# Output projection of a decode step: result on 16 rows of 112 columns, pairs batch first, more heads in the 448-wide sum

## The chip, the cores and the metric

The kernel runs on one core of a Trainium2 chip. A core has a matrix engine (TensorE, here PE; its weight loads are listed apart as PEld), a vector engine (VectorE, DVE), a scalar engine (ScalarE, ACT), a general engine (GpSimd, POOL) and an engine that mainly issues transfers (SyncE, SP). They run their own programs and meet at semaphores. Sixteen DMA engines move data between the memory outside the core (HBM) and the on-chip memory SBUF; matmuls write into PSUM, which has eight banks of 128 partitions by 512 fp32 columns. The metric is the device time of one execution in microseconds (us).

## The reference

Four sequences, one new token each, with a cache of 8192 keys and values for 8 key/value heads of width 256; two query heads share a key/value head, so there are 16 query heads. The model width is D = 448.

```python
xn = layernorm(x)                                        # x: 4 x 1 x 448
q = (xn @ wq)                                            # 448 x 4096: 16 heads of 256
scores = einsum("bhqd,bhkd->bhqk", q, k) * 256**-0.5     # k, v: 4 x 8 x 8192 x 256
o = einsum("bhqk,bhkd->bhqd", softmax(scores), v)
s = o.reshape(4, 1, 4096) @ wo                           # 4096 x 448
h2 = gelu(layernorm(xn) @ w3) @ w4                       # 448 -> 1792 -> 448
g = silu(xn + h2)
return x + s * g
```

The reference has another branch in the MLP, over shifted groups of channels. With one token per sequence every shift leaves only zeros, so it adds nothing and the kernel leaves it out. K and V are 268 MB in bf16; all else is about 10 MB.

## The kernel before, in words

**Pairs.** The 32 (batch, key/value head) combinations are worked on in 16 pairs of neighbouring heads of one batch (`where`, line 141, says which). A pair's K is 8 MB and lies in SBUF with 64 partitions for each head, 128 positions in each partition. PE transposes K in groups of eight 128x128 blocks (`f_t`, line 650), DVE and ACT copy the groups to `kT` (`evac`, line 348), PE multiplies them by the query (`f_s`, line 663), ACT takes the exponential (`exps`, line 372), and PE multiplies by V (`f_pv`, line 700). DVE divides by the sum of the exponentials and writes the attention output, transposed, to `OT_all` (`f_ot`, line 545), eight columns for each pair: two heads by two halves of the head's width by two query heads. The loop over the pairs runs with a delay: V of one pair is used while K of the next is worked on.

**Queues.** SP issues every large load in order (`prog_sp`, line 236): wq, w3, the first K, w4, the part of wo for heads 9 to 15, then K and V of the pairs, and at the end V of the last pair in five pieces and the rest of wo in the order of `LATE` (line 126): heads 0 and 1, 2 and 3, 4 and 5, 6 and 7, then head 8 in two halves. Loads wait for buffers by semaphores that DVE raises (`v_k`, `v_v`). w4 lies where wo's heads 0 to 8 come later, so those heads can't be loaded before the MLP is done (`v_w4`).

**The MLP** runs between the eighth and the ninth pair (`mlp`, line 633, on PE; `f_mlp`, line 491, on DVE). Its second matmul is summed in four column groups of PE at once; DVE copies the four partial sums to `ou_f` and PE adds them by two fp32 matmuls with a selection matrix `selb`, one for each 224 columns of the result. That gives the result's form: the first 224 columns on partitions 0 to 3, the others on partitions 32 to 35. x and the normalized x are copied to the same form (`x4`, `xn4`, line 501).

**The output projection** (`finish`, line 765). Each of the 16 heads has two halves of 128 rows in `wo_sb`. Heads 9 to 11 are multiplied 448 columns wide in four column groups (`f_ou`, line 734), DVE copies the four partial sums to `ou_f` (line 581), and PE adds them by `selb` into the result in PSUM bank `o_ps` (line 779) after the first piece of the last V. The other heads go straight to `o_ps` (`f_o`, line 745): two matmuls of 224 columns for each half of a head, one for each group of partitions. Heads 12 to 15 (from `ALONE`, line 732) need the last pair's attention output; heads 0 to 8 need their late weights. DVE then multiplies by the gate `sg4` (line 593), adds x (line 595), and SP and ACT each store one half.

## Time and profile before

| | us |
|---|---|
| median of 4 runs (652.62 to 652.96) | 652.75 |
| the profiled execution | 652.69 |
| its span, first to last instruction | 651.1 |

| engine | busy us | share of the span |
|---|---|---|
| PE matmul | 503.3 | 77% |
| PEld (weight loads) | 412.1 | 63% |
| DVE | 257.5 | 40% |
| ACT | 269.0 | 41% |
| POOL | 3.7 | 1% |

The DMA engines moved 279.13 MB, 429 GB/s over the span. Busy shares are averages over the span; what a change at the end is worth is read in the chain of work that ended last and in the timeline there. In the timeline a row has its start and its length in us, then the engine, the line, the operation, what it writes and reads, the shapes, and in brackets how long the engine had been idle and what ended that. "PEq" and "DVEq" are those engines' sequencers, which take the waits at line 321. The windows give for a stretch of time its length, the busy time of PE, PEld, DVE, ACT and POOL (in brackets the number of instructions), PE's granted clock, the mean busy share of the DMA engines and the rate in GB/s. Matmuls of different column groups run side by side, so their lengths overlap.

### The profile page before, as it was taken

Reading aid. Unit: us, or ns where it says so; the run is one execution under the profiler, and the core shown is the slowest. Engines: PE = TensorE matmul, PEld = TensorE weight load, DVE = VectorE, ACT = ScalarE, POOL = GpSimd, SP = SyncE. Lnnn points to the kernel's source line nnn. Section 1 sums busy time; section 2 is a strip of 40 time slices with the busy share of each in tenths; the row PEclk is TensorE's granted clock in tenths of the full one; section 3 lists DMA queues with packets and bytes.
Section 4 is the critical chain, followed back from the end, with each engine's and each line's share of the span. In section 5 each row is a group of like instructions: output and inputs, shape, how many; then the busy total and the mean of one; then the engine's idle time right before and its main releaser. Section 6 shows DMA issues by size and latency. Waiting matters only on the chain. (4 is left out here: it accounts for less than half of the span.)

```text
span 651.1 us, 22042 instructions
## 1 busy us (share of the span) xinstructions
PE 503.3 (77%) x9699; PEld 412.1 (63%) x9699; DVE 257.5 (40%) x507; ACT 269.0 (41%) x361; POOL 3.7 (1%) x18
## 2 busy tenths in 40 slices
PE   2979979595877958588589868959597695959856
PEld 1876959294774928568277765919477392856824
DVE  7434535252442525335154343515244252433511
ACT  6634626062542605345144543606344260543510
POOL 2000000000000000000000000000000000000000
PEclk9778989697996969889689898969799796988968
DMA  9999999999999999999999999999999999999997
GB/s 387 443 421 424 439 431 451 419 440 429 437 447 407 463 407 459 409 453 431 423 448 413 457 413 439 441 427 443 423 443 443 411 455 415 443 427 433 453 405 302
DMA packets 10801, 279.13 MB, mean 429 GB/s; under 512 B 1060, under 2 KB 3240, under 8 KB 3752
## 3 DMA queue, kind: packets, MB, share of 16 engines
q1 hardware_dynamic: 10776, 278.99, 99.5%
q8 instruction: 7, 0.11, 0.1%
q14 instruction: 2, 0.02, 0.0%
q10 hardware_dynamic: 16, 0.01, 0.0%
HBM read 278.99 MB, written 0.00 MB: 428 GB/s over the span
## 5 line engine op out<-in xcount | busy, mean ns | idle before, releaser
L658 PE MATMUL pst<-ident_b,kn 128*128 128x128 bf16 x4096 | 304.6, 222 | 26.9 <-PEq L321 25.5
L355 ACT ACTIVATE kT<-pst 128x1024 bf16<-128x1024 bf16 x224 | 226.4, 1023 | 122.6 <-ACTq L321 122.5
L353 DVE COPY kT<-pst 128x1024 bf16<-128x1024 bf16 x288 | 197.8, 692 | 178.6 <-DVEq L321 178.6
L658 PEld LDWEIGHTS pst<-ident_b,kn 128*128 128x128 bf16 x4096 | 242.1, 99 | 28.9 <-issue 28.9
L671 PE MATMUL psc<-qc,kT 128*128 128x4 bf16 x4096 | 174.1, 165 | 6.3 <-PEq L321 5.8
L703 PE MATMUL psv<-vb,pT 128*8 128x512 bf16 x1024 | 103.6, 503 | 92.9 <-PEq L321 92.9
L671 PEld LDWEIGHTS psc<-qc,kT 128*128 128x128 bf16 x4096 | 153.4, 97 | 34.6 <-issue 34.2
L379 ACT ACTIVATE pT<-psc,negb 64x128 bf16<-64x128 f32 x64 | 28.4, 535 | 236.6 <-ACTq L321 236.3
L703 PEld LDWEIGHTS psv<-vb,pT 128*8 128x8 bf16 x1024 | 24.9, 94 | 125.9 <-issue 115.3
L514 DVE TENSOR_REDUCE rmax<-psc 64x2 f32<-64x256 f32 x32 | 13.5, 422 | 130.9 <-DVEq L321 130.7
L696 PE MATMUL psm<-sel,po 128*128 128x4 f32 x136 | 18.4, 258 | 1.4 <-PEq L321 1.4
L696 PEld LDWEIGHTS psm<-sel,po 128*128 128x128 f32 x136 | 17.3, 196 | 1.5 <-issue 1.5
L379 ACT ACTIVATION_READ_ACCUMULATOR pT<-psc,negb 64x1 f32 x64 | 16.4, 256 | 0.0
L543 DVE COPY po<-psv 128x512 f32<-128x512 f32 x17 | 11.8, 692 | 9.4 <-DVEq L321 9.4
L535 DVE COPY negb<-psm 128x4 f32<-128x4 f32 x16 | 2.6, 162 | 30.1 <-DVEq L321 30.1
L524 DVE TENSOR_REDUCE gmax<-psm 2x2 f32<-2x128 f32 x16 | 4.5, 278 | 20.5 <-DVEq L321 20.5
L367 ACT ACTIVATE vb<-pT 128x5000 bf16<-128x5000 bf16 (+2 forms) x3 | 10.6, 3568 | 0.1
L684 PEld LDWEIGHTS psm<-diag,ones_f 2*128 2x128 f32 x32 | 4.7, 182 | 7.0 <-issue 7.0
L680 PEld LDWEIGHTS psm<-ident_f,rmax 128*2 128x2 f32 x16 | 1.3, 81 | 12.3 <-issue 12.3
L603 PE MATMUL pst<-ident_b,xn_b 4*128 4x4 bf16 x14 | 0.6, 161 | 9.4 <-DVE xn_b L428 9.3
L603 PEld LDWEIGHTS pst<-ident_b,xn_b 4*128 4x128 bf16 x14 | 0.5, 95 | 10.3 <-issue 9.3
L703 PE MATMUL psv<-kn,pT 128*8 128x512 bf16 x58 | 5.6, 514 | 1.3 <-PEq L321 1.3
(93 smaller groups left out, 88.5 us busy)
## 6 DMA issues: line engine op xcount, KB each, us to landing
kn<-in_A_k_cache_dram SPq DMA_DIRECT2D x30, 4096.0 KB, 26.4
kn<-in_A_k_cache_dram SPq DMA_DIRECT2D x4, 2048.0 KB, 16.3
vb<-in_A_v_cache_dram SPq DMA_DIRECT2D x2, 4096.0 KB, 20.3
kn<-in_A_v_cache_dram SPq DMA_DIRECT2D x1, 4096.0 KB, 27.7
vb<-in_A_wq_dram SPq DMA_DIRECT2D x1, 3584.0 KB, 11.1
kn<-in_A_v_cache_dram SPq DMA_DIRECT2D x1, 2048.0 KB, 26.2
wo_sb<-in_A_wo_dram SPq DMA_DIRECT2D x4, 448.0 KB, 26.7
vb<-in_B_w_dram SPq DMA_DIRECT2D x1, 1568.0 KB, 13.7
```

Of the source, the lines that this page charges most:

```text
L353: engine.tensor_copy(dst, src).then_inc(S["v_ev"], 1)
L355: engine.activation(dst, src, ACT.Copy).then_inc(S["a_ev"], 1)
L367: f = act.activation(t, pT[:, 0:1].broadcast_to([P, t.shape[1]]), ACT.Copy)
L379: ins = act.activation(pT[own, 0:NC2 * NR].rearrange("p (c n) -> p n c", n=NR)[:, n], psc[own, 0:NC2 * NR].rearrange("p (c n) -> p n c", n ...
L514: ins = v.tensor_reduce(rmax[own, :], psc[own, 0:NC2 * NR].rearrange("p (c n) -> p n c", n=NR)[:, t * REP:(t + 1) * REP], AX.X, ALU.max)
L524: v.tensor_reduce(gmax[:, :], psm[0:REP, 0:P].rearrange("p (s k) -> p s k", s=NS), AX.X, ALU.max).then_inc(S["v_s"], 1)
L543: v.tensor_copy(po[:, :], psv[:, 0:CP * DH]).then_inc(S["v_po"], 1)
L658: ins = pe.transpose(dst[:, n * P:(n + 1) * P], kn[:, t, GC * j + kl, half * P:(half + 1) * P], ident_b[:, :])
L671: ins = pe.matmul(psc[:, kk * NR:(kk + 1) * NR], kT[:, j % RING, n * P:(n + 1) * P], qc[:, :, half, :], start=(half == 0), stop=(half == N ...
L684: pe.matmul(psm[:, P:P + NR], ones_f[0:REP, :], diag[:, :], start=True, stop=True).then_inc(S["p_m2"], 1)
L696: ins = pe.matmul(psm[:, o:o + NR], po[:, i * DH + dh:(i + 1) * DH:NHALF], sel[:, i, 0:NR], start=(i == 0), stop=(i == CP - 1))
L703: ins = pe.matmul(psv[o:o + CP * NR, 0:CP * DH], pT[:, kk * NR:(kk + CP) * NR], src[:, kk:kk + CP, :].rearrange("p c d -> p (c d)"), start ...
```

## The change

The result now has 16 rows of 112 columns: 8 rows (batch by the two halves of 224 columns) on partitions 0 to 7 with the first 112 columns of each half, and 8 on partitions 32 to 39 with the others. Rows of one batch are neighbours. To steer a product to the right one of the two rows, the weights' columns are taken from `OT_all` with a zero column between each two batches' columns: starting at a batch's column, or one step before it. For that, pairs go batch first (pair i is batch i % 4, heads 2 * (i // 4) and the next), and a pair's eight columns in `OT_all` are followed by eight zeros. `selb` likewise has zero columns, and is taken at two offsets. x is loaded to the new form by two transfers on ACT's queue; the normalized x is added before the MLP's partial sums are added. Heads 0 to 3 and 12 to 15 join the 448-wide sum of heads 9 to 11; its copy and the fp32 sum come after them. Heads 4 to 8 go straight to the result, with four matmuls of 112 columns for each half of a head. Heads 6 and 7 are two loads.

```diff
-    LATE = ((0, 1), (2, 3), (4, 5), (6, 7), (8,))
+    LATE = ((0, 1), (2, 3), (4, 5), (6,), (7,), (8,))
     def where(i):
-        return NS * i // HKV, NS * i % HKV
+        return i % Bn, i // Bn * NS
...
+        def ot(hq, dh, m, n=None):
+            k, t = divmod(hq // REP, NS)
+            at = first + k * Bn * NSL * PW + t * TW + dh * REP + hq % REP
+            step = PW
+            if n is None:
+                step = NSL * PW
+            else:
+                at -= n * PW
+            return OT_all[:, at:at + (m - 1) * step + 1:step]
+
+        def sel_sum(n):
+            return selb[:, NSL - 1 - n:NSL - 1 - n + PQ]
+
+        def split(dram, tile, i):
+            return (dram.rearrange("b (s n) -> (b s) n", s=NSL)[:, i * DS:(i + 1) * DS],
+                    tile[i * PQ:i * PQ + NSB, :])
...
         def store(eng, i):
-            eng.dma_start(out2d[:, i * DQ:(i + 1) * DQ], out_b[i * PQ:i * PQ + Bn, :]
-                          ).then_inc(S["dout"], 16)
+            eng.dma_start(*split(out2d, out_b, i)).then_inc(S["dout"], 16)
...
                 c(act.activation(st[:, col + 2:col + 3], st[:, col + 1:col + 2], ACT.Sqrt))
+                for i in range(NDG if k == 2 else 0):
+                    act.dma_start(*split(x2d, x4, i)[::-1]).then_inc(S["dx4"], 16)
...
-            c(v.tensor_reduce(selb[:, :], ident_f[:, :].rearrange("p (j r) -> p r j", j=NQD),
-                              AX.X, ALU.add))
+            c.sync()
+            c(v.tensor_reduce(selb[:, NSL - 1:NSL * Bn + NSL - 1:NSL], ident_f[:, :].rearrange(
+                "p (j r) -> p r j", j=NQD)[:, 0:Bn], AX.X, ALU.add))
...
-                c(v.tensor_copy(
-                    qT[:, :, :, dh, hh].rearrange("p b (a i) -> p i a b", a=NHF),
-                    qt_ps[:, m * P:(m + 1) * P].rearrange("p (i n) -> p i n", i=NQD)[
-                        :, :, 0:NHF * Bn].rearrange("p i (a b) -> p i a b", a=NHF)))
+                for t in range(NS):
+                    c(v.tensor_copy(
+                        qT[:, :, :, t, dh, hh].rearrange("p (a j) b -> p j a b", a=NHF),
+                        qt_ps[:, m * P:(m + 1) * P].rearrange("p (j s n) -> p s j n", s=NS, j=NQD // NS)[
+                            :, t, :, 0:NHF * Bn].rearrange("p j (a b) -> p j a b", a=NHF)))
...
-                v.tensor_copy(ou_f[:, :], h2_ps[:, 0:D]).then_inc(S["v_h2"], 1)
-                for src, dst in ((x_f, x4), (xn_f, xn4)):
-                    for i in range(NDG):
-                        ins = v.tensor_copy(dst[i * PQ:i * PQ + Bn, :],
-                                            src[:, i * DQ:(i + 1) * DQ])
-                ins.then_inc(S["v_s"], 1)
+                v.tensor_copy(ou_f[:, :], h2_ps[:, 0:D]).then_inc(S["v_s"], 1)
                 take(v, "v_s")
+                v.tensor_tensor(ou_f[0:Bn, :], ou_f[0:Bn, :], xn_f[:, :], ALU.add
+                                ).then_inc(S["v_h2"], 1)
+                v.wait_ge(S["dx4"], 16 * NDG)
                 take(v, "p_hs")
-                v.tensor_tensor(bout[:, :], hs_ps, xn4[:, :], ALU.add).then_inc(S["v_w"], 1)
+                v.tensor_copy(bout[:, :], hs_ps).then_inc(S["v_w"], 1)
...
-                    OT_all[:, bass.ds(at, PW)].rearrange("p (s a r) -> p a s r", s=NS, a=NHALF),
+                    OT_all[:, bass.ds(at * NSL, PW)].rearrange("p (s a r) -> p a s r", s=NS, a=NHALF),
...
             turned(NH * TW).then_inc(S["v_ot"], 1)
-            take(v, "p_ou")
-            v.tensor_copy(ou_f[:, :], ou_ps[:, 0:D]).then_inc(S["v_a"], 1)
             f_rz()
...
                 :, :, 0:NR]).then_inc(S["v_ot"], 1)
+            take(v, "p_ou")
+            v.tensor_copy(ou_f[:, :], ou_ps[:, 0:D]).then_inc(S["v_a"], 1)
             v.wait_ge(S["p_o"], 1)
-            c(v.tensor_tensor(res[:, :], o_ps[0:DP, 0:DQ], sg4[:, :], ALU.mult))
+            c(v.tensor_tensor(res[:, :], o_ps[0:DP, 0:DS], sg4[:, :], ALU.mult))
...
+            def f_sums(dst, start, stop):
+                for n in range(NSL):
+                    for i in range(NDG):
+                        at = n * DQ + i * DS
+                        ins = pe.matmul(dst[i * PQ:(i + 1) * PQ, 0:DS], sel_sum(n),
+                                        ou_f[:, at:at + DS], start=start and n == 0,
+                                        stop=stop and n == NSL - 1)
+                return ins
...
+            SUMMED = [hq for hs in LATE[:2] for hq in hs]
+            NOU = (HQ - NLATE + len(SUMMED)) * NHALF
+            nth = []
             def f_ou(hs):
                 for hq in hs:
                     for dh in range(NHALF):
-                        k = (hq - NLATE) * NHALF + dh
-                        o = k % NCG * CGW
-                        ins = pe.matmul(ou_ps[o:o + PQ, 0:D], OT[:, hq // REP, hq % REP, dh, :],
+                        k = len(nth)
+                        nth.append(hq)
+                        o, m = k % NCG * CGW, PQ if k < NCG else Bn
+                        ins = pe.matmul(ou_ps[o:o + m, 0:D], ot(hq, dh, m),
                                         wo_sb[:, hq, dh, :], start=(k < NCG),
...
-                        for i in range(NDG):
-                            ins = pe.matmul(o_ps[i * PQ:(i + 1) * PQ, 0:DQ],
-                                            OT[:, hq // REP, hq % REP, dh, :],
-                                            wo_sb[:, hq, dh, i * DQ:(i + 1) * DQ], start=False,
-                                            stop=stop and hq == hs[-1] and dh == NHALF - 1)
+                        for n in range(NSL):
+                            for i in range(NDG):
+                                at = n * DQ + i * DS
+                                ins = pe.matmul(o_ps[i * PQ:i * PQ + NSB, 0:DS],
+                                                ot(hq, dh, NSB, n),
+                                                wo_sb[:, hq, dh, at:at + DS], start=False,
+                                                stop=stop and dh == NHALF - 1 and n == NSL - 1)
...
-                f_ou(range(NLATE, ALONE)).then_inc(S["p_ou"], 1)
+                f_ou(range(NLATE, ALONE))
...
-                    if i == 0:
-                        take(pe, "v_a")
-                        for n in range(NDG):
-                            pe.matmul(o_ps[n * PQ:(n + 1) * PQ, 0:DQ], selb[:, :],
-                                      ou_f[:, n * DQ:(n + 1) * DQ], start=True, stop=False)
...
                 take(pe, "dwl0", 16)
-                f_o(LATE[0])
+                f_ou(LATE[0])
                 take(pe, "v_ot")
-                f_o(range(ALONE, HQ))
-                for i in range(1, len(LATE) - 1):
+                f_ou(range(ALONE, HQ))
+                take(pe, "dwl1", 16)
+                f_ou(LATE[1]).then_inc(S["p_ou"], 1)
+                take(pe, "v_a")
+                f_sums(o_ps, True, False)
+                for i in range(2, len(LATE) - 1):
                     take(pe, "dwl%d" % i, 16)
                     f_o(LATE[i])
```

`first` is 32, two pairs' room ahead of the first pair's columns; NSL = 2, DS = 112, NSB = 8. `x4` is now bf16, `xn4` is gone, and `x4`, `sg4`, `res`, `bout` and `out_b` are 112 columns wide.

## The prediction

> **What bounds the kernel now.** I read the share of the DMA engines first, then the chain that ended last, then the timeline of the last 17 us, then where the last weights land.
>
> ```profile
> DMA  9999999999999999999999999999999999999997
> q1 hardware_dynamic: 10776, 278.99, 99.5%
> 647.50:648.00 0.50, 0.11 (x2) 0.14 (x4) 0.00 (x0) 0.00 (x0) 0.00 (x0) 1.00 0.17 56
> 648.00:649.00 1.00, 0.81 (x12) 0.53 (x11) 0.15 (x1) 0.00 (x0) 0.00 (x0) 1.00 0.00 0
> ```
>
> SP's queue keeps the DMA engines busy for 99.5% of the span, in every slice but the last; 278.99 MB stand against 651.1 us. Two windows near the end show the data stopping at about 648.0 us. So only three things can move the time: the rate of the stream, a hole in it, and the 3.1 us between the end of the data and the end of the span. The chain shows those:
>
> ```profile
> 647.89 0.94 PE pst L749 x12
> 648.83 0.02 issue
> 648.85 0.39 DVE res L593
> 649.27 0.38 DVE out_b L595
> ```
>
> ```profile
> 634.55 0.60 PE L739 MATMUL pst<-wo_sb,OT_all 128*32 128x448 bf16 x6 [0.46 <-PEq L321]
> 635.30 0.63 DVE L581 COPY ou_f<-pst 128x448 f32<-128x448 f32 x1 [0.89 <-DVEq L321]
> 638.69 0.47 PE L779 MATMUL pst<-ou_f,selb 128*32 128x224 f32 x2
> 639.00 0.36 PE L779 MATMUL pst<-ou_f,selb 128*32 128x224 f32 x2
> 644.21 0.35 PE L759 MATMUL pst<-pT,kn 128*128 128x32 bf16 x8
> 644.49 1.90 PE L749 MATMUL pst<-wo_sb,OT_all 128*32 128x224 bf16 x32
> 646.76 0.60 PE L749 MATMUL pst<-wo_sb,OT_all 128*32 128x224 bf16 x8 [0.36 <-PEq L321]
> 647.89 0.93 PE L749 MATMUL pst<-wo_sb,OT_all 128*32 128x224 bf16 x12 [0.53 <-PEq L321]
> 649.68 0.35 SPq L233 DMA_DIRECT2D out_dram<-out_b  x1
> ```
>
> These timeline rows give the prices: six 448-wide matmuls 0.60 us, the copy of the sum 0.63, two fp32 matmuls of 224 columns 0.67 from first start to last end (each is two passes), a 224-wide matmul 49 ns after the one before ((0.60 - 0.26) / 7; one alone lasts 259 ns), a 32-wide one 25 ns ((0.35 - 0.176) / 7). PE sits idle before each group at L749: it waits for weights. L312's two loads are issued at 638.03 and 640.03 and land 10.0 and 8.3 us later (longest and shortest in that line's answer), at 648.0 and 648.3; L299's last, heads 6 and 7, lands 17.2 us after 630.53, at 647.7, the one before at about 646.6. The last two of the twelve load their weights at 648.47, 0.1 us after the ten before them: **the end hangs on the landing of head 8's second half**.
>
> **The change, part by part.**
>
> 1. *The last landing.* The bytes are the same; heads 6 and 7 become two loads of 224 KB. Between L299's landings a 448 KB load takes 1.13 us, and L312's 112 KB 0.3, so 224 KB cost between 0.56 and 0.6: two are 0 to 0.07 us more. I take +0.03. SP issues one load more (0.4 to 0.5 us where it isn't held up); its last issue today lies 8.3 us ahead of its landing, so that is covered. The residual x comes as two 1.8 KB loads (16 rows of 224 B) on ACT's queue at about 12 us: at the stream's 429 GB/s 0.01 us, at worst 0.1 if they delay the slowest engine.
>
> 2. *PE behind that landing.* Four matmuls of 112 columns in place of two of 224. Two column groups run side by side; 112 columns stream in half of 224's time, and a pair of 224 takes 2 x 49 = 98 ns, so 112 columns fewer are 47 to 49 ns fewer: one lasts 259 - 47 = 212 ns. The last starts 50 to 75 ns after the first and ends 0.02 us earlier than now: -0.02, ends -0.05 and +0.1.
>
> 3. *Is PE free by then?* This is the step on which the forecast turns. Now PE has only direct matmuls here. The wait for DVE's copy of the sum, today after the first piece of V and met before PE comes to it, moves behind heads 2 and 3: all direct matmuls are queued behind it on PE, and DVE's last multiply behind those. DVE's own wait for the sum moves behind its last OT, with only that multiply after it. Heads 0 to 3 and 12 to 15 join the 448-wide sum: heads 0, 1 (4 matmuls), then, after DVE's last OT at 644.88, heads 12 to 15 (8), then heads 2, 3 (4), landed at 645.5 (618.41 + 27.1). The 16 cost less than today's 32 (1.90 us): by L739, four are 0.41 us from first start to last end. So the sum ends at 645.62 + 0.41 = 646.03. DVE starts 0.15 us later (today 635.15 to 635.30), copies 0.63, to 646.81; PE starts 0.15 after that (as in the MLP: copy ends 327.48, first matmul 327.62), at 646.96. Four fp32 matmuls of 112 columns stream as many columns as L779's two, behind which others may already start: 0.4 to 0.5 us, to 647.4. Then heads 4 to 7 and half of head 8 are 36 matmuls of 112 columns. Nothing in the trace is 112 wide in column groups. The ends: 25 ns (L759's step) and 49 ns (L749's). At 25 PE is done at 648.3, before the wait that ends at 648.47; at 49 at 649.2, with the last four at 649.6. I take 25 to 28: two groups need 24 ns each for 112 columns, loads of 8 weight columns (82 to 88 ns in L703's rows) are shorter than L759's (96), and those already fit in 25. So 0 on the path; the other end is +0.8.
>
> Here a page speaks against the change. The Trainium skill, "TensorE: Matmul & The Clock Gate", section "Back-to-back issue gap", puts a sustained pair of weight load and matmul at about 81 ns for 128 columns. By it PE would end at about 650.8, 2.0 us later than now, and the sum below would be 654.5. L749's 49 ns for 224 columns already undercuts that figure, so I don't go by it.
>
> 4. *DVE at the end.* Two operations on 64x224 (383 and 382 ns) become 64x112. A tensor-tensor of 128x56 takes 216 ns, so a column costs (383 - 216) / 168 = 1.0 ns and 112 columns 272: -0.11 each, -0.22. The ends: 0 (no gain) and -0.33 (both as at 56 columns; x4 is bf16 now).
>
> 5. *The store.* 8 rows of 224 B on each of SP and ACT in place of 4 of 448. From issue at 649.68 to the end of the span are 1.42 us. Rows doubled, bytes equal: +0.05, ends -0.05 and +0.2 (half the 0.35 us of issue again).
>
> 6. *Start.* DVE makes 8 small copies of qT for 4 (four end 0.69 us after the first starts, 19.44 to 20.13): +0.4 us. It is then idle until 21.70, when the first transposes come, which wait for K. ACT issues two loads more (0.28 to 0.56 us each) and its fills slide to 18.9; its first evacuation is at 22.5. Cost 0; with that cover gone it would meet the next: SP issues the next K at 33.20, while what is queued lands until 43.3 (3.63 + 39.7), some 8 us of cover with 2 us for engines that end early. `selb`'s extra wait and memsets end before x lands at 4.5.
>
> 7. *MLP in the middle.* DVE adds the normalized x (4x448, by L445's 0.38 and L418's 0.50 about 0.5 us) between the copy at 326.85 and PE's sum; four copies of 4x224 beside it go. PE, and the transposes queued behind it, come 0.6 to 0.7 us later; who waits is SP's next K, issued at 341.17. The V load of 322.65 runs until about 353: 10 us of cover, cost 0. The multiply of `at` on DVE's registers, 16 times, meets the same cover.
>
> 8. *Pair order.* Each load is as large and as contiguous as before; only its first address changes. The stream already jumps between the K and the V array twice per pair, and no slice shows a hole. K loads are issued at 180.10, 219.07, 257.42 and 296.13, 38.7 apart on average. I take 0; the ends have no nearer row than the windows of 20 us, which run between 412 and 454 GB/s, so a change of either sign can't be excluded; 0.2% either way is 0.09 us per pair.
>
> Also, 16 KB instruction fetches (7 on their queue, about 0.9 us each on one engine) may be one more or fewer: the one at 332 us made the landings around it 0.3 late. I take 0, ends -0.3 and +0.3.
>
> **Sum.** +0.03 - 0.02 + 0 - 0.22 + 0.05 = -0.16 us. The profiled execution took 652.69 (span 651.1 and 1.6 around it), the median shown 652.75; the same few tenths come off either: 652.75 - 0.16 = **652.6 us**.
>
> **Rivals.**
>
> *PE is behind.* The narrow matmuls keep L749's step, or the fp32 sum starts late. For it: PE stands idle from 646.0 to 646.9 while heads 4 and 5 land at 646.6, and afterwards has 40 matmuls where 20 are left now. Against it: L759's 25 ns. Time at 49 ns: +0.8 - 0.16 = +0.6, 653.4. It decides from about 30 ns a matmul (36 x 30 = 1.08 us, to 648.5).
>
> *The stream is slower in the new order* (the other side). One mechanism: the jump of a batch at each load costs the queue time. 0.1 us at each of 15 jumps is +1.5 - 0.16: 654.1. It decides from 0.09 us a pair; for it stands only that 20 us windows differ by a tenth; against it that the K/V jumps show no hole.
>
> *The stream ends earlier.* The engines end unevenly: the DMA share is 0.86, 0.56, 0.47 and 0.17 in the last four half microseconds, 0.97 us of idle engines. If other fetches or small loads even that out, up to -1.0 - 0.16: 651.6; with a faster stream less. Nothing in the change aims its bytes at single engines.
>
> *The narrow operations save nothing.* DVE's fixed part rules, and the doubled rows cost what they may: 0 + 0.2, 652.9.
>
> **How the numbers follow.** What a measurement here can tell from no change is about 0.2%, 1.3 us: faster ends at 651.4, slower begins at 654.1. The forecast with the rival of no saving has 0.56, its own range 652.2 to 653.0. PE behind: 0.20, of it 0.03 beyond 654.1. The slower stream: 0.13, 0.10 beyond. The earlier end: 0.11, 0.07 beyond. So faster 0.07, same 0.80, slower 0.13. Leaving out 0.1 at either end gives 651.6 to 654.1.
>
> **What would show it.** In the changed profile: L593's and L595's successors at 0.27 us; the copy of the sum at about 646.2 and the fp32 sum at 647.0; the last four matmuls alone, after an idle gap of PE that the last landing ends; that landing at 648.3 to 648.4; K issues 38.7 apart. Wrong would be: no idle PE from 647 on (PE behind); a DMA share under 9 or K issues further apart (the stream); a last landing off by over 0.3 us.

## Result and profile after

Before: 652.71 us, median of 62 executions (652.58 to 653.14). The changed kernel: 653.43 us, median of 41 (652.15 to 654.92), ratio 1.0009 [1.0005, 1.0013]. So the median is 0.1% slower, with the whole interval above 1, where 652.6, a little faster, was forecast. One thing must be known to read these numbers: the executions of the changed kernel lie in three groups, those of the kernel before in one, so its median goes with the shares of the groups.

```
                 executions   around
before           62           652.71   (652.58 to 653.14)
changed, first   19           652.41   (652.15 to 652.60)
changed, second   7           653.54   (653.33 to 653.67)
changed, third   15           654.45   (654.15 to 654.92)
```

The profiled execution of the changed kernel took 652.50 us with a span of 651.0, and belongs to the first group. On its page the stream is as dense as before:

```profile
DMA  9999999999999999999999999999999999999997
...
q1 hardware_dynamic: 10800, 278.99, 99.5%
q8 instruction: 7, 0.11, 0.1%
```

The windows at its end (length; busy time of PE, PEld, DVE, ACT, POOL with counts; PE's clock; DMA share; GB/s):

```profile
647.50:648.00 0.50, 0.50 (x27) 0.50 (x22) 0.00 (x0) 0.00 (x0) 0.00 (x0) 1.00 0.26 86
648.00:649.00 1.00, 0.90 (x25) 0.54 (x19) 0.03 (x1) 0.00 (x0) 0.00 (x0) 1.00 0.01 4
```

PE is busy throughout the half microsecond from 647.5, where it had 0.11 us of work before. The chain that ended last (start, length, what):

```profile
647.06 0.58 PE pst L655 x8
647.64 0.99 PE pst L781 x36
648.63 0.03 issue
648.65 0.29 PE pst L781 x4
648.94 0.02 issue
648.97 0.28 DVE res L611
649.25 0.02 issue
649.27 0.27 DVE out_b L613
```

It begins at the fp32 sum (`f_sums`, L655) and has all 40 direct matmuls (L781) in it; before, it began 0.9 us from PE's end. The timeline shows the same end with what is not on the chain:

```profile
645.38 0.74 PE L769 MATMUL pst<-wo_sb,OT_all 128*4 128x448 bf16 x12 [0.17 <-PEq L337]
646.29 0.62 DVE L609 COPY ou_f<-pst 128x448 f32<-128x448 f32 x1 [1.05 <-DVEq L337]
647.06 0.58 PE L655 MATMUL pst<-ou_f,selb 128*32 128x112 f32 x8 [0.93 <-PEq L337]
647.44 1.49 PE L781 MATMUL pst<-wo_sb,OT_all 128*8 128x112 bf16 x40
648.62 0.14 PEld L781 LDWEIGHTS pst<-wo_sb,OT_all 128*8 128x8 bf16 x4 [0.16 <-issue]
648.97 0.27 DVE L611 TENSOR_TENSOR res<-pst,sg 64x112 f32<-64x112 f32 x1 [2.06 <-PE pst L781]
649.56 0.37 SPq L250 DMA_DIRECT2D out_dram<-out_b  x1
```

This is the end that was forecast: 36 narrow matmuls are done when the last weights land at 648.52, and four follow them alone. Against before: the last landing is 0.15 later (648.37), PE's end behind it 0.04 shorter, DVE's two operations 0.23 shorter, the store the same 1.42 us; 0.15 - 0.04 - 0.23 = -0.12, which is what the span lost (651.10 to 650.98). The first of the four starts 240 ns after the last of the 36, where a matmul otherwise follows after 24.5, so PE has waited some 0.2 us; in the profile of e1_again below it is 61 ns, and PE and the landing come almost together. If the first group is like these profiles, the forecast's mechanism held in 19 of 41 executions. What the other 22 do, this profile can't show. The experiments had to find it.

### The profile page after: what moved, and what is told of

Same layout as the page of the kernel before. It is cut to its first block, busy times and chain, and to the rows that moved or that the text cites. A ratio compares the mean times of both kernels' runs of the same rounds, so it can differ in the third digit from the quotient of the medians.

```text
span 651.0 us, 22071 instructions
## 1 busy us (share of the span) xinstructions
PE 498.5 (77%) x9711; PEld 408.7 (63%) x9711; DVE 256.4 (39%) x508; ACT 268.6 (41%) x361; POOL 3.4 (1%) x18
## 5 line engine op out<-in xcount | busy, mean ns | idle before, releaser
L683 PE MATMUL pst<-ident_b,kn 128*128 128x128 bf16 x4096 | 301.5, 221 | 25.1 <-PEq L337 23.6
L683 PEld LDWEIGHTS pst<-ident_b,kn 128*128 128x128 bf16 x4096 | 239.6, 99 | 26.6 <-issue 26.6
L713 PE MATMUL psw<-rowsum,ones_f 128*128 128x4 f32 x34 | 6.7, 269 | 0.0
```

The costliest lines, as they stand in the source:

```text
L683: ins = pe.transpose(dst[:, n * P:(n + 1) * P], kn[:, t, GC * j + kl, half * P:(half + 1) * P], ident_b[:, :])
L713: pe.matmul(psw[:, 0:NR], ones_f[:, :], rowsum[:, :], start=True, stop=True).then_inc(S["p_s"], 1)
```

## Experiments

### What makes the groups: order of the pairs, x loads, or stores?

The first theories took three parts of the change that touch the queues: the new order of the pairs (theory O), the two small loads of x on ACT's queue with DVE's wait for them (theory X), and the stores with 16 rows of 224 B in place of 8 of 448 (theory S). Each was undone alone beside the changed kernel itself. These four share a before of 652.76.

**e1_again** is the changed kernel without an edit.

> The changed kernel as it is, for its spread. Its 43 executions so far lie in three groups: about 652.4 (21), 653.5 (7) and 654.5 us (15), while the kernel before stays within 652.58 to 653.14. I expect the three groups again, in about these shares. If the profiled execution falls in a slow group, its tail tells where the time is: theory X (the small x loads on ACT's queue hold up one DMA engine) expects the last landing 1 to 2 us after 648.5 and the rest as before; theory C (PE's clock is granted at half in the tail of some executions) expects a granted clock near 0.5 after 643 us and the last landing at 648.5; theory S (the stores of 224 B rows, which share lines of the output between the two queues) expects all as before up to 649.6 and a longer end.

Measured: 652.45 (652.30 to 653.78); nine of 11 executions in the first group, 653.55 and 653.78 in the second. The groups come in changing shares, and the ratio to before with them: 0.9998 [0.9989, 1.0007] here. None of these 11 lies in the third group. (The 43 that the expectation counts are the 41 above and two more of the first group.)

**e1_no_x_load** leaves the two loads and the wait out, so x isn't added.

```diff
-                for i in range(NDG if k == 2 else 0):
-                    act.dma_start(*split(x2d, x4, i)[::-1]).then_inc(S["dx4"], 16)
...
-                v.wait_ge(S["dx4"], 16 * NDG)
```

> The two x loads and the wait for them are left out, so x isn't added to the result. Theory X: one group alone, near 652.4. Theories C, S and O (the batch-first order disturbs the stream): the same three groups, median 653 to 654.

Measured: 652.55 (652.21 to 655.0); eight of 11 in the first group, three at 654.3, 654.42 and 655.0. The third group is there without the loads: theory X falls.

**e1_old_order** takes the pairs in the old order.

```diff
     def where(i):
-        return i % Bn, i // Bn * NS
+        return NS * i // HKV, NS * i % HKV
```

> The pairs' order of before with everything else of the change; queries and outputs then belong to other pairs than the keys, the work is the same. Theory O: one group, near 652.4. Theories X, C and S: three groups as in the changed kernel.

Measured: 652.98 (652.13 to 654.49); six of 12 in the first group, one at 653.42, five from 654.09 on. Theory O falls.

**e1_half_store** stores only the first 112 columns of each half; the rest of the result stays unwritten.

```diff
         def store(eng, i):
-            eng.dma_start(*split(out2d, out_b, i)).then_inc(S["dout"], 16)
+            eng.dma_start(out2d[:, i * DQ:i * DQ + DS], out_b[i * PQ:i * PQ + Bn, :]).then_inc(S["dout"], 16)
```

> Each store writes 4 rows of 224 B, 448 or more apart from the other store's (the other half of the output is left unwritten). Theory S: one group, near 652.4. Theories X, C and O: three groups as in the changed kernel, each at most 0.1 us earlier.

Measured: 653.94 (652.24 to 654.95); four of 12 in the first group, two in the second, six in the third. Theory S falls.

None of the three parts makes the groups. But the profiled execution of e1_old_order was one of the third group (654.09), and its timeline shows where the time goes:

```profile
644.95 1.82 PE L769 MATMUL pst<-wo_sb,OT_all 128*4 128x448 bf16 x16
646.93 0.62 DVE L609 COPY ou_f<-pst 128x448 f32<-128x448 f32 x1 [1.60 <-DVEq L337]
647.70 0.96 PE L655 MATMUL pst<-ou_f,selb 128*32 128x112 f32 x8 [0.93 <-PEq L337]
648.42 2.10 PE L781 MATMUL pst<-wo_sb,OT_all 128*8 128x112 bf16 x40
650.56 0.27 DVE L611 TENSOR_TENSOR res<-pst,sg 64x112 f32<-64x112 f32 x1 [3.00 <-PE pst L781]
```

Its last weights land at 648.31, earlier than in the profile after. Yet DVE's last multiply starts 1.59 us later. The sum's copy is 0.64 later (646.93 against 646.29), the direct matmuls start 0.72 after the fp32 sum instead of 0.38 (+0.34), and they take 2.10 instead of 1.49 (+0.61). A direct matmul comes (2.10 - 0.29) / 39 = 46.4 ns after the one before, where the other profile has 24.5. PE works at about half its rate; the copy on DVE takes the same 0.62. The windows, cut where the clock changes, say why (the figure behind the engines is PE's granted clock):

```profile
636.73:640.14 3.41, 3.41 (x36) 1.02 (x28) 0.20 (x1) 0.00 (x0) 0.00 (x0) 0.50 0.96 408
640.14:643.55 3.41, 1.89 (x34) 1.09 (x30) 0.69 (x1) 0.00 (x0) 0.00 (x0) 1.00 1.02 401
643.55:646.97 3.42, 3.22 (x31) 1.73 (x30) 0.20 (x2) 0.00 (x0) 0.00 (x0) 0.50 0.98 372
646.97:650.38 3.41, 2.68 (x48) 2.58 (x48) 0.59 (x1) 0.00 (x0) 0.00 (x0) 0.50 0.11 38
```

In all traces of this case the clock is either 0.5 or 1.0, and changes only at steps 3.41 us apart, whose place against the program's start differs from execution to execution (643.55 here, 644.35 in the profile after). The Trainium skill, "TensorE: Matmul & The Clock Gate", section "Part 1: The HAM clock gate", describes just this: two levels, decided by the array's activity in free-running windows of 3413 ns. The traces agree.

### Is it the clock?

The new theory: in some places of the steps, PE streams too little in one step of the changed tail, the clock halves, and the end runs at half speed. Its rival: PE is late for another reason, and the clock only goes with it. Two kernels keep PE busy or idle with nothing else changed; a third undoes the later sum. Before here: 652.85.

**e2_keep_busy** adds matmuls whose result nobody reads, where PE waits.

```diff
+            def f_idle(n):
+                for _ in range(n):
+                    pe.matmul(pst[2][:, 0:512], ident_b[:, :], kT[:, 0, 0:512], start=True, stop=True)
...
+                    f_idle(2 if i == 2 else 0)
                     take(pe, "dvl%d" % i, 16)
...
+                f_idle(2)
                 f_direct(NPIECE - ND)
...
                 f_ou(LATE[1]).then_inc(S["p_ou"], 1)
+                f_idle(3)
                 take(pe, "v_a")
```

> The changed kernel with seven matmuls of 128x512 into an unused PSUM bank while PE waits: two before the third piece of V, two before the fourth, three while DVE copies the sum. Theory C: the groups at 653.5 and 654.5 get rarer or vanish, the fast group stays near 652.4 (at half clock seven of them are 3.0 us, so some executions may lose some tenths). Any theory in which the clock is a bystander: the three groups stay as they are.

Measured: 652.57 (652.32 to 653.31), ratio to before 0.9997 [0.9988, 1.0006]; seven of 11 up to 652.57, four from 653.0 to 653.31, none near 654.4. That alone proves little, as e1_again had none there either; taken with the two runs below that fill the same three waits with less (e4_fill_113, e5_fill_113), one of 33 executions lies in the third group, against 15 of 52 of the changed kernel (41 and e1_again). More work on PE makes the group rare, which a PE that is late by its work can't explain. The fill has a price: the profiled execution (653.31) is at full clock from 641.56 on, yet its copy of the sum starts 1.12 us after that of the profile after (646.29):

```profile
644.00:648.00 4.00, 3.77 (x53) 2.23 (x51) 1.36 (x3) 0.00 (x0) 0.00 (x0) 1.00 0.81 305
647.41 0.62 DVE L609 COPY ou_f<-pst 128x448 f32<-128x448 f32 x1 [1.05 <-DVEq L337]
```

**e2_idle_after** leaves out the multiplication of the first three pieces of the last V but for four matmuls, so that PE stands idle for 3.88 us ahead of the third piece, which it reaches at 641.46 as in e1_old_order (641.40).

```diff
                     take(pe, "dvl%d" % i, 16)
-                    ins = f_pv(kv, PIECES[i], PIECES[i + 1], pb)
+                    if i == NPIECE - ND - 1:
+                        ins = f_pv(kv, 0, NCG * CP, NCG * CP)
```

> The same left out in the changed kernel. Theory C: nearly all executions in the slow groups, 653.3 to 655, median about 654.4. If the clock is a bystander: three groups with the shares of the changed kernel, about half at 652.4.

Measured: 654.54 (654.33 to 654.73), ratio 1.0026 [1.0016, 1.0036]. With less work all eight executions lie in the third group, and its windows show half the clock from 634.66 to the end:

```profile
634.66:638.07 3.41, 2.45 (x14) 1.56 (x13) 0.36 (x3) 0.80 (x5) 0.00 (x0) 0.50 0.96 411
638.07:648.00 9.93, 4.95 (x54) 3.05 (x56) 1.95 (x5) 0.00 (x0) 0.00 (x0) 0.50 0.93 366
648.00:651.00 3.00, 2.77 (x48) 2.50 (x48) 0.19 (x1) 0.00 (x0) 0.00 (x0) 0.50 0.00 0
```

Its last weights land at 648.37, no later than in the profile after. So the third group is the tail at half clock.

**e2_idle_before** is the same edit in the kernel before (same diff).

> The kernel before with its multiplication by the first three pieces of the last V left out but for four matmuls, so PE idles from about 635 to 641 us and comes into the tail at half clock in most executions. Theory C: the 52 matmuls of 224 columns keep PE busy enough to get the clock back, and 8 of 12 lie behind the landing at 647.8; 652.8 to 653.6, less than 1 us over the kernel before. If the kernel before never loses by half clock, 652.7.

Measured: 653.53 (653.13 to 654.79), ratio 1.0012 [1.0003, 1.0021]. In its profile (653.50) the clock is half from 635.22 to 648.88; the median is 0.7 us above before's. The kernel before is not immune to a low clock; it has less behind it at the end. Of its 236 executions in all series, one lies above 653.36 (e3_before below).

**e2_early_sum** takes the sum back to its old place, with heads 9 to 11 alone in it, and keeps the 16 rows.

```diff
-            NOU = (HQ - NLATE + len(SUMMED)) * NHALF
+            NOU = (ALONE - NLATE) * NHALF
...
                     ins = f_pv(kv, PIECES[i], PIECES[i + 1], pb)
+                    if i == 0:
+                        take(pe, "v_a")
+                        f_sums(o_ps, True, False)
...
-                f_ou(LATE[0])
+                f_o(LATE[0])
                 take(pe, "v_ot")
-                f_ou(range(ALONE, HQ))
-                take(pe, "dwl1", 16)
-                f_ou(LATE[1]).then_inc(S["p_ou"], 1)
-                take(pe, "v_a")
-                f_sums(o_ps, True, False)
-                for i in range(2, len(LATE) - 1):
+                f_o(range(ALONE, HQ))
+                for i in range(1, len(LATE) - 1):
```

> The change without its later sum: only heads 9 to 11 are summed 448 wide, copied and added where the kernel before does it; heads 0 to 3 and 12 to 15 go straight to the result with matmuls of 112 columns. Theory C (the granted clock: a profile in the slow group showed 0.50 from 643.6 to 650.4 us, changes 3.41 us apart, and the last landing not later) in its form 'the later sum thins PE's work between 643 and 647 us, so the gate keeps half the clock, and leaves more work behind it': one group near 652.4 to 652.5 or a spread of some tenths as in the kernel before. If instead the 16-row form is at fault (twice as many matmuls in the end), the three groups stay, median 653 to 654.5.

Measured: 653.97, 654.24, 666.28, 667.08, 667.14 and 671.65. This doesn't answer the question, as it brought a cost of its own. Its 104 direct matmuls in place of 40 make PE's program longer, and the page of the shortest execution counts ten instruction fetches of 16 KB in place of seven:

```profile
q8 instruction: 10, 0.16, 0.1%
```

One of them, at 647.6, falls into the end. The last weights land at 649.43, 0.9 us later than in the profile after, and the clock is full from 642.57 on. In the chain PE then stands for 0.55 us in "issue", waiting for nothing that the profile shows:

```profile
646.61 2.69 PE pst L781 x95
649.30 0.55 issue
649.85 0.56 PE pst L781 x9
```

That the fetches make the gap and the late landing is argued from the place of the one; for the 666 to 672 us of four other executions even that is missing, as none of them was profiled. How the 16 rows alone would do stays open.

### Which part of the change lowers the clock?

Now the later sum was put alone into the kernel before, and the fill of e2_keep_busy was split. Before here: 652.71.

**e3_late_sum**: heads 0 to 3 and 12 to 15 in the 448-wide sum, copy and fp32 sum behind them; result on 8 rows, old order, old stores.

```diff
-            take(v, "p_ou")
-            v.tensor_copy(ou_f[:, :], ou_ps[:, 0:D]).then_inc(S["v_a"], 1)
             f_rz()
...
-                    if i == 0:
-                        take(pe, "v_a")
-                        for n in range(NDG):
-                            pe.matmul(o_ps[n * PQ:(n + 1) * PQ, 0:DQ], selb[:, :],
-                                      ou_f[:, n * DQ:(n + 1) * DQ], start=True, stop=False)
...
-                f_o(LATE[0])
+                f_ou(LATE[0])
                 take(pe, "v_ot")
-                f_o(range(ALONE, HQ))
-                for i in range(1, len(LATE) - 1):
+                f_ou(range(ALONE, HQ))
+                take(pe, "dwl1", 16)
+                f_ou(LATE[1]).then_inc(S["p_ou"], 1)
+                take(pe, "v_a")
+                for n in range(NDG):
+                    pe.matmul(o_ps[n * PQ:(n + 1) * PQ, 0:DQ], selb[:, :],
+                              ou_f[:, n * DQ:(n + 1) * DQ], start=True, stop=False)
+                for i in range(2, len(LATE) - 1):
```

> One part of the change alone, on the kernel before: heads 0 to 3 and 12 to 15 join the 448-wide sum, whose copy and fp32 sum come after heads 2 and 3. Result still on 4 rows of 224 in two groups, pairs in the old order, 224-wide matmuls. Theory C with the later sum as its cause: groups appear, the fast one at 652.6 to 652.8, slow ones 1 to 2 us above. If the 16-row form is the cause: one group at 652.7 as in the kernel before.

Measured: 654.59 (652.58 to 655.31), ratio 1.0019 [1.001, 1.0029]; three of 11 around 652.6, two around 653.8, six from 654.59 on. All three groups come with this part alone. The windows of its profile (654.82):

```profile
639.93:643.34 3.41, 1.75 (x35) 0.79 (x27) 0.69 (x1) 0.00 (x0) 0.00 (x0) 1.00 1.02 401
643.34:646.75 3.41, 3.41 (x32) 2.50 (x32) 0.17 (x1) 0.00 (x0) 0.00 (x0) 0.50 1.00 381
646.75:650.17 3.42, 2.48 (x27) 1.77 (x22) 0.62 (x1) 0.00 (x0) 0.00 (x0) 0.50 0.13 46
```

**e3_wait_fill**: of the fill only three matmuls, ahead of the third piece of V.

```diff
+                    f_idle(3 if i == 2 else 0)
                     take(pe, "dvl%d" % i, 16)
```

> The changed kernel with three matmuls of 128x512 into an unused PSUM bank before the wait for the third piece of V (0.64 us at full clock), none elsewhere. If the gate drops at 643 to 644 us because PE waited through most of the 3.41 us before: the slow groups vanish or get rare, fast group 652.4, some executions 0.1 to 0.6 later. If the thin work after 644 us is what matters alone: the groups stay.

Measured: 653.41 (652.56 to 654.34), ratio 1.0012 [1.0003, 1.0021]; one of 11 at 652.56, six around 653.4, four around 654.2. Its profile (654.21) shows the thin step moved to the copy of the sum, 644.24 to 647.65:

```profile
640.83:644.24 3.41, 2.90 (x48) 1.16 (x41) 0.69 (x1) 0.00 (x0) 0.00 (x0) 1.00 1.03 399
644.24:647.65 3.41, 2.33 (x32) 1.55 (x32) 0.78 (x2) 0.00 (x0) 0.00 (x0) 1.00 0.86 322
647.65:651.06 3.41, 2.83 (x48) 2.58 (x48) 0.36 (x3) 0.00 (x0) 0.00 (x0) 0.50 0.01 4
```

**e3_copy_fill**: only two matmuls, while DVE copies the sum.

```diff
                 f_ou(LATE[1]).then_inc(S["p_ou"], 1)
+                f_idle(2)
                 take(pe, "v_a")
```

> The changed kernel with two such matmuls while DVE copies the sum, none elsewhere. The gate has dropped before that, so the groups stay in number; where the two make the stretch to 647 us dense enough for the clock to come back, the group at 654.5 moves towards 653.5. If the waits before 643 us don't matter: the groups vanish.

Measured: 652.79 (652.35 to 654.16), ratio 1.0003 [0.9994, 1.0012], spread from one end to the other. In its profile (653.17) the clock halves at 645.61 and is full again at 649.03.

**e3_before** is the kernel before as it is, to find its steps.

> The kernel before, for its profile. In its profile so far the clock's changes lay at 638.9, 642.3, 645.7 us and it stayed full. If this execution has changes near 640.1 and 643.5 (as the slow one of the changed kernel had): theory C expects half the clock from 643.5, full again at about 647, and a time within 0.5 us of 652.7.

Measured: 652.88 (652.40 to 654.06). In its profile (652.85) the steps lie at 641.65, 645.06 and 648.48, and the clock is full from the first on. Of eight executions one took 654.06, which stays unexplained.

No profile of the changed kernel itself fell into the second group; that it comes from a drop at a later step or a shorter one, as in e3_copy_fill, is argued, not shown. e3_wait_fill dropped later too, at 647.65, and took 654.21; e2_keep_busy took 653.31 at full clock. What makes the second group stays open.

So neither fill does it alone: the change leaves two thin places, the wait for the third piece, which the fp32 sum has left, and the copy of the sum.

### Does the kernel before meet the same steps?

One sub-theory was that the kernel before drops too and recovers in time. The second question was how little fill suffices. Before here: 652.82.

**e4_before_a** and **e4_before_b** are the kernel before as it is.

> The kernel before once more, for the clock of its tail. If the gate's steps fall near 640.1 and 643.5 us: either it drops there too and is full again at about 647 (then the dense matmuls of 224 columns give it back, and the time stays within 0.5 us of 652.7), or it doesn't drop (then the work to 643.5 differs).

> The same kernel, for another position of the steps: with steps near 644.3 and 647.7 us I expect full clock throughout, as in the changed kernel's fast profile.

Measured: 652.80 (652.65 to 653.07) and 652.75 (652.58 to 653.01). By luck e4_before_a has its steps where the third-group e1_old_order has them:

```profile
636.73:640.14 3.41, 3.41 (x38) 1.58 (x32) 0.57 (x2) 0.00 (x0) 0.00 (x0) 0.50 0.97 409
640.14:643.55 3.41, 2.24 (x37) 1.11 (x31) 0.69 (x1) 0.00 (x0) 0.00 (x0) 1.00 1.03 403
643.55:646.97 3.42, 3.04 (x52) 2.70 (x53) 0.17 (x1) 0.00 (x0) 0.00 (x0) 1.00 0.98 372
646.97:650.38 3.41, 1.29 (x20) 0.82 (x16) 0.77 (x2) 0.00 (x0) 0.00 (x0) 1.00 0.10 36
```

Same places, same clock until 643.55, and then 1.00 where e1_old_order has 0.50: here the kernel before doesn't drop, nor in its three other profiles (steps at 642.33, 641.65 and 639.79). So the sub-theory falls for these places of the steps; for others no profile shows it. Its timeline shows why the step from 640.14 has more in it:

```profile
638.47 0.59 PE L779 MATMUL pst<-ou_f,selb 128*32 128x224 f32 x2
...
638.84 0.59 PE L779 MATMUL pst<-ou_f,selb 128*32 128x224 f32 x2
638.91 1.80 PE L703 MATMUL psv<-kn,pT 128*8 128x512 bf16 x14
641.44 0.81 PE L703 MATMUL psv<-kn,pT 128*8 128x512 bf16 x10 [0.73 <-PEq L321]
```

The fp32 sum between the pieces, itself at half clock, pushes the second piece of V to 640.71; in e1_old_order it ends at 640.32, and PE is idle for 1.08 us ahead of the third piece instead of 0.73.

How much a step holds can be worked out from the trace: 112 columns more make a matmul 259 - 212 = 47 ns longer, so a column takes 0.42 ns at full clock (twice that at half, and again twice in fp32, which makes two passes); each matmul's streaming lies that long ahead of its end less the 0.165 us that remain of 212. The time in which any matmul streams, over the steps between two possible changes:

```
profile          step (us)        clock   streamed   clock in the next step
e1_old_order     640.14-643.55    1.0     0.93       0.5
e5_fill_203      640.51-643.92    1.0     0.96       0.5
e3_late_sum      639.93-643.34    1.0     1.01       0.5
e3_wait_fill     644.24-647.65    1.0     1.08       0.5
e3_copy_fill     642.20-645.61    1.0     1.09       0.5
e4_before_a      640.14-643.55    1.0     1.29       1.0
e1_old_order     633.31-636.72    1.0     1.30       0.5
e4_fill_113      642.44-645.86    1.0     1.30       1.0
e4_before_b      639.79-643.20    1.0     1.44       1.0
after            644.35-647.77    1.0     1.63       1.0
e3_before        624.58-628.00    0.5     2.37       0.5
e1_old_order     646.96-650.38    0.5     2.64       1.0
e3_copy_fill     645.61-649.03    0.5     2.66       1.0
```

The gate's bound lies near 1.3 of 3.41 us on the way down, and between 2.4 and 2.6 on the way up. These are estimates: with 0.160 us for the 0.165 some entries rise by up to 0.06, so hundredths say nothing. But the same working over all 3,698 steps of the 20 profiles bears them out. Of 2,728 steps at full clock, every one below 1.19 us lost it and every one above 1.32 kept it; of 970 at half clock, every one below 2.37 stayed there and every one above 2.55 came back. The exact bounds stay open. The kernel before stood at 1.29 here, at the bound itself.

**e4_fill_113** is e2_keep_busy with one, one and three matmuls.

```diff
-                    f_idle(2 if i == 2 else 0)
+                    f_idle(1 if i == 2 else 0)
...
-                f_idle(2)
+                f_idle(1)
                 f_direct(NPIECE - ND)
```

> The changed kernel with five filling matmuls: one before the third piece of V, one before the fourth, three while DVE copies the sum. Theory C: no group at 654.5; fast group 652.4, the others at most 0.5 to 1 above; median 652.4 to 652.6.

Measured: 652.59 (652.33 to 652.99), ratio 0.9997 [0.9988, 1.0005]: one group, level with before.

**e4_sum_no23** has heads 2 and 3 straight to the result instead, and three fill matmuls in the copy.

```diff
-            SUMMED = [hq for hs in LATE[:2] for hq in hs]
+            SUMMED = [hq for hs in LATE[:1] for hq in hs]
...
-                f_ou(range(ALONE, HQ))
-                take(pe, "dwl1", 16)
-                f_ou(LATE[1]).then_inc(S["p_ou"], 1)
+                f_ou(range(ALONE, HQ)).then_inc(S["p_ou"], 1)
+                f_idle(3)
                 take(pe, "v_a")
                 f_sums(o_ps, True, False)
-                for i in range(2, len(LATE) - 1):
+                for i in range(1, len(LATE) - 1):
```

> The changed kernel with heads 2 and 3 straight to the result, so the sum's copy starts about 0.45 us earlier (at 645.75 for 646.2), and three filling matmuls during the copy. At full clock the end is the same, 652.4, since the last landing sets it. At half clock 56 narrow matmuls of 47 ns follow the fp32 sum for 40: 0.75 us more against 0.45 less. Slow group at 654.5 to 655 in the steps that drop at 643.5, unless the filling brings the clock back at 647: then 653 to 653.5.

Measured: 653.34 (652.42 to 654.61), ratio 1.0011 [1.0002, 1.0019]; five of 12 from 652.42 to 652.67, five from 654.29 on. The groups stay, which fits the wait for the third piece left thin; the profiled execution (652.55) is of the fast ones and doesn't show the drop.

### A place for the fill, and the fill again

Before here: 652.92.

**e5_fill_203** puts two fill matmuls behind the first piece, where the kernel before has its fp32 sum, and three in the copy.

```diff
-                    f_idle(1 if i == 2 else 0)
+                    f_idle(2 if i == 1 else 0)
                     take(pe, "dvl%d" % i, 16)
...
-                f_idle(1)
                 f_direct(NPIECE - ND)
```

> The changed kernel with two filling matmuls after the first piece of V, where the kernel before had its fp32 sum, and three during the copy. In the profiles so far the clock dropped after steps in which PE streamed 0.94 to 1.27 us of 3.41, and stayed after 1.32 and more. By that rule the two lift the step that ends at 643.6 from 0.94 to about 1.4 and the three the one that ends at 646.8 from 1.1 to about 1.7: no group at 653.5 or above, median 652.4 to 652.6. If the rule is wrong: groups as in the changed kernel.

Measured: 652.99 (652.34 to 654.55), ratio 1.0002 [0.9993, 1.0011]; two executions at 654.5. In the profiled one (654.55) the step from 637.09 ran at full clock, so the two fills were soon over and lay ahead of the thin step:

```profile
637.09:640.51 3.42, 2.38 (x37) 0.68 (x30) 0.15 (x1) 0.00 (x0) 0.00 (x0) 1.00 0.97 407
640.51:643.92 3.41, 1.84 (x31) 1.21 (x31) 0.69 (x1) 0.00 (x0) 0.00 (x0) 1.00 1.03 401
643.92:647.33 3.41, 3.08 (x31) 1.72 (x32) 0.41 (x2) 0.00 (x0) 0.00 (x0) 0.50 0.92 348
```

The place was wrong; the step's 0.96 us of streaming stands with the others in the table. The expectation's 1.27 and 1.32 are the table's 1.30 (e1_old_order) and 1.29 (e4_before_a), too near to each other to tell apart.

**e5_fill_113** repeats e4_fill_113 without an edit.

> The kernel with one, one and three filling matmuls again, for a narrower interval: 652.3 to 653.0, median 652.5 to 652.6, 0.1 to 0.3 us under the kernel before.

Measured: 652.64 (652.39 to 654.60), ratio 0.9999 [0.999, 1.0008]; ten of 11 up to 652.84, one at 654.60. With e4_fill_113, 21 of 22 executions are free of the slower groups, against 28 of 52 of the changed kernel. The fill brings the change back to the level of before; that it beats it is not shown.

## Why the prediction was right or wrong

**1, the last landing** (+0.03). It came at 648.52 in the profile after, +0.15. But 0.14 of this is there before the split: the first piece of the last V lands at 641.47 for 641.33, heads 4 and 5 at 646.76 for 646.62. From there to head 7 it takes 1.14 us with two loads and 1.13 with one, so the split cost 0.01. The landing itself moves more than that from profile to profile (648.27 to 648.58, e2_keep_busy with 648.85 and e2_early_sum apart).

**2 and 3 at full clock.** A narrow matmul lasts 213 ns in the median (212 forecast) and comes 24.5 ns after the one before where PE doesn't wait (25 to 28). The copy of the sum starts at 646.29 (646.18), the fp32 sum at 647.06 (646.96), the direct matmuls at 647.44 (647.4); the last four wait for the landing, though by only some 0.2 us here and almost nothing in e1_again. The steps taken from L759's row were right. The 81 ns a pair that the Trainium skill, "TensorE: Matmul & The Clock Gate", section "Back-to-back issue gap", gives for 128 columns, and that the forecast had weighed against them, doesn't hold for 112 columns in two column groups side by side, with weights of 8 columns: the trace has 24.5 ns.

**3, "Is PE free by then?", is the step that failed.** Every duration in it was at full clock, from one profile whose clock was 1.00 from 638.9 on. Whether it would stay there was not asked. The step moved the fp32 sum away from the wait for the third piece, halved the work from 644.5 to 646.4 (32 matmuls of 1.90 us become 16), put an idle PE behind it (0.93 us), and left 40 matmuls and the sum behind that. The first three make steps of the clock thin enough to halve it, the fourth makes PE the bound when it does. In the step's own terms: the 36 matmuls got the upper end of 49 ns (46.4 measured), and the copy and the fp32 passes, for which no upper end was given, were 0.64 and 0.34 us later. So what the sum took as "0 on the path" was 1.59 us in the profiled execution of e1_old_order against the profile after: there PE, and not the landing, set the end. e3_late_sum shows that this part of the change suffices for the groups. The changed kernel itself has no profile from its slow groups, but with the later sum the five profiled executions from 654.09 up all end at half clock (e1_old_order, e2_idle_after, e3_late_sum, e3_wait_fill, e5_fill_203), and the seven up to 652.55 all at full clock.

**4**: the two DVE operations take 268 and 267 ns (272). **5**: issue to the end of the span 1.42 us, as before (+0.05). **6**: the eight copies of qT take 0.79 us, the K load issued at 33.20 goes out at 34.55, inside the 8 us of cover. **7**: the K load issued at 341.17 goes out at 340.16, no later. **8**: K loads go out at 180.26, 218.78, 257.46 and 296.34, (296.34 - 180.26) / 3 = 38.7 us apart, as forecast; seven instruction fetches as before.

**The sum.** -0.16 was forecast; the profile's span gives -0.12, the first group's median -0.30. As a forecast of what happens when the clock stays full it holds, in the mechanism; its size of a few tenths is no larger than the spread of before (652.58 to 653.14).

**The rivals.** "PE is behind" (0.20, 653.4) came true for the third group, 15 of 41 executions at about 654.4, as far as e1_old_order stands for it; for the seven near 653.5, its very figure, nothing shows it. Its step of a matmul was right and its cause not: the narrow matmuls don't keep L749's step, they run at half clock, so the figure was met partly by luck. It should have had half of the chance, and 654.4 as its far end. "The stream is slower in the new order" and "the narrow operations save nothing" did not happen; of "the stream ends earlier" no run shows a sign.

## What to carry to other kernels

A tail that waits for data has PE's clock at stake: before work there is packed tighter or moved, add up what PE streams in 3.4 us, for every place that the steps may take, and price the end at half clock too. One profiled execution shows one place of the steps; the times of all executions show the others, as groups. Where the work is too thin, a few matmuls that nobody reads, placed in the waits, can hold the clock; the fill has to lie in the thin step itself.

## What the runs showed of the hardware

- PE need not be idle for long to lose the clock. In e1_old_order the longest gap in the step ahead of the drop was 1.08 us. The Trainium skill, "TensorE: Matmul & The Clock Gate", section "Why this matters for your kernels", asks only that gaps between bursts of matmuls stay under some 3 us; here a step with 0.93 us streamed and no such gap halved the clock, and the measurement decides.
- Down and up have different bounds: about 1.3 us of 3.41 keeps a full clock, about 2.5 is needed to get it back (estimates from the table and from all steps).
- Matmuls side by side in column groups seem to count as one in this: packing the same products into four groups takes activity from the step. Weighted by the share of the array that they use, the steps don't fall in order: over all steps of the 20 profiles as little as 0.31 us kept the clock and as much as 1.32 lost it. Counted once, the two sides overlap only from 1.19 to 1.32.
- A longer PE program may cost far more than its matmuls: e2_early_sum, with 64 more direct matmuls and ten fetches in place of seven, lay between 653.97 and 671.65. That the fetches cost it is not shown.
